# A planned kernel for an FFT mixer with a gated feed-forward: whole accumulator banks as the unit of a wait, no pauses in the weight preparation, a later deadline, longer loads

## The chip, the core and the metric

The kernel runs on one core of a Trainium2 chip. The core has a matrix engine (TensorE, called PE; its weight loads are listed apart as PEld), a vector engine (DVE), an activation engine (ACT), a general engine (POOL) and a queue that issues transfers (SP). Each takes its own instructions in the order in which the program holds them and waits for the others by semaphores. Matrix products land in accumulator banks (PSUM, 512 f32 values per partition and bank, eight banks), from which DVE and ACT read. The metric is the device time of one execution in microseconds.

## The reference, cut to what matters

For x of 8192 tokens by 448 channels, all in f32:

```
xn = layernorm(x)
s  = irfft2(soft(mlp2(relu(mlp1(rfft2(xn))))))   # complex block MLP over the frequencies, 4 blocks of 112 channels, soft threshold 0.01
g  = silu((gelu(xn @ w_gate) * (xn @ w_up)) @ w_down)   # 448 -> 1792 -> 448
out = x + s * g
```

The transform runs along the 8192 tokens only (the other spatial axis has length 1). It is computed as two stages of 128 and 64 points. Precision close to f32 comes from splitting every operand into two f16 parts and making three products of them.

## The kernel before

**Two streams.** The feed-forward (ffn() and chunk()) is the main stream on PE. It takes the 8192 tokens in 16 chunks of 512, twice: pass p=0 with the first 8 of the 14 column blocks of w_gate and w_up, pass p=1 with the other 6. The first two chunks of p=0 are computed plainly; every later one uses seven products instead of eight for the 2x2 block product of x with the weights (unit(), product()), on tokens and weights whose sums were made beforehand. Each chunk ends with its down projection onto 448 columns. Its partial result goes to DRAM (prt) in p=0 and is taken up again in p=1 (pt).

**The down projection** comes in two forms. The plain one, down(), is for each of four token tiles a run of 8 blocks x 3 matmuls of 448 columns in p=0. The other, down2() with prod2(), makes seven products instead of eight, of 224 columns each; it needs extra sums of the activations (sums() in unit(), which keeps them in the tiles "left" and "right" and in h) and factors of w_down (factors2(), factors_in()). chunk() chooses this form as soon as state holds "left", which prep_mlp() puts there with its last lines. At the start of the first such chunk, factors_in(0) loads the factors of w_down over the plain weights. All of p=1 uses it.

**The other stream** runs beside it in three phases. Phase 1 normalises x, makes the first transform stage (chunk1(), stage1()) and the sums of x; phase 2 (phase2(), group()) makes the second stage, the block MLP (layer1()), the threshold and the first inverse stage, in 16 groups of frequencies times 4 channel blocks, 64 in all; phase 3 (phase3(), tiles3(), load3()) makes the last inverse stage, multiplies with the gate and adds x. When phase 3 begins, chunks of p=1 that are past have left their gate in DRAM (gsp) and phase 3 reads it back, two loads for each; chunks that follow (from state["direct"] on) multiply at once, in gate().

**The weights** are prepared beside phase 1 by weights(): scaled, split and summed, for p=0 at the start and from some 150 us later for p=1 (gu_block() with 1), then the factors of w_down for p=1 (down_weights(1)) and for p=0 (factors0()), then the block MLP's weights (prep_mlp()).

**The order is planned while the program is built.** Pace is a small event simulation: every task is a generator that yields a time, an event, or nothing (wait until the last issued operation is done). issue() estimates the start and end of each operation and appends it to its engine's program at that moment, so the estimated times set the order in which instructions stand in each queue. They set nothing on the chip, where the semaphores rule. Four parts matter here:

- region(), ready() and note() say which earlier operations one has to wait for in the planner's model: operations on the same tensor whose column ranges overlap, a read only for writes, a write for both.
- The branch for SP in issue() estimates when a transfer has landed: 2.2 us and its size at 240 GB/s, or the end of the queue's traffic, and 2.5 us more for loads after 100 us.
- END2 and END3 are due times: phase 2 spaces the 64 groups evenly between its begin and END2, phase 3 its tiles between its begin and END3.
- calm() holds a task of the preparation back until its engine is free.

Rings (Ring.get and put) hand out buffers; a task without one waits. In layer1() one bank (BF) holds two sums: p0 in columns 0 to w and p1 in columns 256 to 256 + w. ACT copies p0 to k (common()), PE makes p1 meanwhile, DVE adds p1 to k (other()), and 1 us after the copy PE adds the third product to p0.

In the profile all operations carry line 200, the one line through which issue() records them, so they are told apart by their tiles: bx, by, bd and bf are the banks; wt and dw the weights; xta and xtb the transposed x; h the activations; z, zs, wn, vt and u belong to phase 2.

Of the kernel before, what the change touches and what calls it, by code (L numbers as in the profile page):

```python
# [16 lines left out]
PSUM = bass.MemoryType.PSUM  # L17
# [4 lines left out]
NG = 16  # L22
# [27 lines left out]
class Pace:  # L50
# [37 lines left out]
    def run(self):  # L88
        while self.heap:
            t, _, task = heapq.heappop(self.heap)  # L90
            self.now = max(self.now, t)
            self.last = self.now
            try:
                y = next(task)
            except StopIteration:
                continue
            if isinstance(y, Event):
                if y.done:
                    self.push(task, self.now)
                else:  # L100
                    y.waiting.append(task)
            else:
                self.push(task, self.last if y is None else max(self.now, y))


    @staticmethod
    def region(ap):
        dims = list(ap.ap)
        lo = ap.offset % max(1, dims[0][0])
        return ap.tensor.name, lo, lo + sum((n - 1) * s for s, n in dims[1:]) + 1  # L110
# [22 lines left out]
    def issue(self, e, op, out, ins, run):  # L133
        outs, ins, start = self.start(e, out, ins)
        if e == "SP":
            size = (outs or ins)[0].nbytes()
            self.dma = max(self.dma, start) + size / 320e3
            if op == "dma_start_transpose":
                self.free[e] = start + 1.15 + size / 380e3
                end = max(self.free[e] + 2.6, self.dma + 1.5)  # L140
            else:
                self.free[e] = start + 0.5
                end = max(start + 2.2 + size / 240e3, self.dma + 1.5) + (2.5 if outs and start > 100.0 else 0.0)
        else:
            end = start + self.cost(e, op, start, out, ins)
            self.free[e] = end
            if self.shares(e, op, out, ins):
                self.port[e] = self.port[e][-11:] + [(start, end)]
        for i in ins:
            self.note(i, False, end, e)  # L150
        for o in outs:
            self.note(o, True, end, e)
        self.last = max(self.last, end)
        return run()
# [233 lines left out]
def afno_geglu_kernel(ctx, tc, x, gu, wd, mlp, b1, b2, c_m, c_mt, c_small, out):  # L388
    nc = tc.nc
    pace = Pace()  # L390
# [86 lines left out]
    def ev(*key):  # L477
        return EV.setdefault(key, Event())

    def done(*key):  # L480
        pace.set(ev(*key))
# [176 lines left out]
    T1, DT = 84.0, 38.0  # L658


    def gu_loads(fs, again):
        for f in fs:
            t = yield from WS.get()
            if f < 4 and not again:
                yield 2.5 + 2.5 * f

            n = (8 if f < PF[0][1] and not again else SL) * 128
            Q.dma_start(t[:, 0:n], gu[f][:, 0:n])
            EV["wst", f, again] = t.rearrange("p (s c) -> p s c", s=SL)
            pace.then(lambda f=f: done("wl", f, again))  # L670
# [15 lines left out]
    def gu_block(b, to):  # L686

        f0, n = BLK[b]
        for i in range(n):
            yield ev("wl", f0 + i, 0)  # L690
            t = EV["wst", f0 + i, 0]
            yield from calm("DVE")
            V.tensor_reduce(fm[:, i, :, b], t[:, 0:8].rearrange("p (i k) f -> p i (k f)", i=2),
                            axis=AXIS.X, op=ALU.max, apply_absolute_value=True)
            yield
        mx = fx[:, :, b]
        if n == 2:
            V.tensor_tensor(mx, fm[:, 0, :, b], fm[:, 1, :, b], op=ALU.max)
        else:
            V.tensor_copy(mx, fm[:, 0, :, b])  # L700
        yield
        yield from largest(fx[:, :, NBK + b], mx, 2.0 ** -30)
        scales(b)
        yield
        scales_of_products(b)
        done("scales", b)
        for i in range(n):
            f = f0 + i
            t = EV["wst", f, 0]
            if to == 0:  # L710
                d, k = wt[f], 0
            else:
                d, k = (yield from WO.get()), 2
            yield from gu_split(f, t, d, k)
            done("w", f)
            if to == 0:
                WS.put(t)
            if i == 0:
                scale_of_gate(b)
            if to == 1:  # L720
                yield from gu_comb(f, t, d[:, :, 8 - k:16 - k])
                Q.dma_start(wsp[f - PF[1][0]], d.rearrange("p s v c -> p (s v c)"))
                WO.put(d)

    def gu_combs(fs):

        yield ev("w", 5)
        pace.spawn(gu_loads(fs, 1))
        for f in fs:
            yield ev("wl", f, 1)  # L730
            yield from gu_comb(f, EV["wst", f, 1], wt[f][:, :, 8:16])
# [53 lines left out]
    def factors2(p, j, v):  # L785

        f = PF[p][0] + 2 * j
        if block(f) == block(f + 1):
            yield from calm("ACT")
            S.activation(v, v, AF.Copy, scale=fd[:, 2, block(f):block(f) + 1])  # L790
        else:
            for e in range(2):
                yield from calm("ACT")
                S.activation(v[:, e], v[:, e], AF.Copy, scale=fd[:, 2, block(f + e):block(f + e) + 1])
        yield
        cb = yield from CB.get()
        c = cb.rearrange("p k c -> p (k c)")[:, 0:4 * DH].rearrange("p (k c) -> p k c", k=4)
        do = yield from WO.get()
        dv = do.rearrange("p s v c -> p s (v c)")[:, :, 0:7 * DH]
        b11, b12, b21, b22 = (v[:, e, DH * c_:DH * c_ + DH] for e in range(2) for c_ in range(2))  # L800
        yield from B.calm("tensor_sub", c[:, 0], b12, b11)
        yield from B.calm("tensor_sub", c[:, 2], b22, b12)
        yield
        yield from B.calm("tensor_sub", c[:, 1], b22, c[:, 0])
        yield
        yield from B.calm("tensor_sub", c[:, 3], b21, c[:, 1])
        yield
        cf = c.rearrange("p k c -> p (k c)")
        for k0, k1, src in ((0, 1, b11), (1, 3, v[:, 1]), (3, 7, cf)):
            yield from calm("ACT")  # L810
            S.copy(dv[:, 0, DH * k0:DH * k1], src)
            yield
            yield from B.calm("tensor_sub", dv[:, 1, DH * k0:DH * k1], src, dv[:, 0, DH * k0:DH * k1])
            yield
        CB.put(cb)
        Q.dma_start(dsp[p][:, :, 7 * DH * j:7 * DH * (j + 1)], dv)
        WO.put(do)

    def factors0(gap):
        for j in range(PF[0][1] // 2):  # L820
            yield pace.now + gap
            t = yield from WS.get()
            v = t[:, 0:2 * D].rearrange("p (t d) -> p t d", t=2)
            Q.dma_start(v, wd[256 * j:256 * j + 256, :].rearrange("(t p) d -> p t d", p=128))
            yield
            yield from factors2(0, j, v)
            WS.put(t)
# [1081 lines left out]

            pace.spawn(store())  # L1910

    END1, END2, END3 = T1 + NG * DT + 12.0, 1410.0, 1765.0

    def phase2():
        yield ev("phase1")
# [265 lines left out]
    def weights():  # L2181

        near = range(PF[0][1])
        t = yield from WS.get()
        Q.dma_start(t[:, 0:8 * 128], gu[1][:, 0:8 * 128])
        EV["wst", 1, 0] = t.rearrange("p (s c) -> p s c", s=SL)
        pace.spawn(gu_loads(near[2:], 0))
        for b in range(1, PB[0][1]):
            pace.spawn(gu_block(b, 0))
            if b == 1:  # L2190
                yield ev("scales", 1)
        combs = pace.spawn(gu_combs(near))
        yield ev("w", 1)
        yield pace.spawn(down_weights(0))
        yield combs
        yield 150.0
        for b in range(*PB[1]):
            yield pace.now + 10.0
            pace.spawn(gu_loads(range(BLK[b][0], sum(BLK[b])), 0))
            yield pace.spawn(gu_block(b, 1))  # L2200
        yield pace.now + 10.0
        yield pace.spawn(down_weights(1))
        yield pace.now + 10.0
        yield pace.spawn(factors0(10.0))
        yield pace.last + 5.0
        yield pace.spawn(prep_mlp())
        done("weights")
# [46 lines left out]
```

## Time and profile before

| | us |
|---|---|
| median of 3 runs | 1802.2 |
| lowest and highest | 1799.91, 1803.22 |
| the profiled execution | 1800.9 |
| its span in the trace | 1799.1 |

A line of instructions in order of time reads: start, duration, engine, line, operation, out<-in, shapes, count of merged instructions, and in brackets the idle time before it with what ended it. The duration of a merged line of matmuls runs to the modelled end of the last one, past the start of what follows, since matmuls overlap; the time that one takes of PE is read from the start of a run to the start of the next line. In a line of waits stand the engine and the tile, what it waited for, and then the total in us, the number of times and the longest. In a line of stages stand the stretch, its length, the busy time of each engine with its number of instructions, and then PE's granted clock as a share of full speed, the share of the 16 transfer engines that was busy, and GB/s.

### The profile page before, as it was taken

To read this page: it belongs to the slowest core of one execution; us is meant where nothing else is said; L and a number is where in the kernel's file an instruction comes from. 1 tells how busy PE (TensorE), PEld (TensorE's weight loads), DVE (VectorE), ACT (ScalarE), POOL (GpSimd) and SP (SyncE) were. 2 spreads that over 40 slices of the span, in tenths; PEclk is the share of its full clock that TensorE was granted. 3 is DMA by queue.
4 is the path that set the end of the run, shared out by engine and by line. 5 is a ranking of instruction groups with operands and counts; after the bars stand their busy time and mean duration, and the time that the engine had idled before them with its cause. 6 is when DMAs were issued, how large, how long until landed. Compare 5 with 4: busy or idle time off the path is not lost. (4 is left out here: it accounts for less than half of the span.)

```text
span 1799.1 us, 39944 instructions
## 1 busy us (share of the span) xinstructions
PE 1759.5 (98%) x16029; PEld 1457.2 (81%) x16029; DVE 1374.8 (76%) x2461; ACT 1012.0 (56%) x1977; POOL 521.5 (29%) x639
## 2 busy tenths in 40 slices
PE   7999999999999999999999999999999999999997
PEld 3446678776787777999999999899989998888887
DVE  7867778776776774777878787888788877888876
ACT  5745556555555544666767666676666653333333
POOL 3333344344433431122213133322223211221111
PEclk9999999999999999999999999999999999999999
DMA  6554775666656633523246555443344349989952
GB/s 219 160 152 126 201 213 158 197 212 185 192 157 202 198 108 107 143 63 73 52 104 197 156 119 120 108 100 95 98 120 117 77 117 305 290 244 287 295 175 63
DMA packets 353802, 283.51 MB, mean 158 GB/s; under 512 B 235120, under 2 KB 324464, under 8 KB 353616
## 3 DMA queue, kind: packets, MB, share of 16 engines
q1 hardware_dynamic: 353328, 280.41, 54.8%
q8 instruction: 125, 2.05, 0.5%
q14 instruction: 61, 0.50, 0.1%
q10 hardware_dynamic: 288, 0.56, 0.1%
HBM read 127.44 MB, written 104.32 MB: 129 GB/s over the span
## 5 line engine op out<-in xcount | busy, mean ns | idle before, releaser
L200 PEld LDWEIGHTS <-wt 128*128 128x128 f16 x9350 | 908.2, 98 | 173.3 <-issue 18.7
L200 PE MATMUL bx<-xta,wt 128*128 128x256 f16 (+1 forms) x3843 | 474.5, 275 | 2.0 <-ACT by L200 1.9
L200 PEld LDWEIGHTS <-h 128*128 128x128 f16 x2708 | 259.7, 98 | 98.4 <-issue 1.9
L200 PE MATMUL bd<-dw,h 128*128 128x448 f16 (+1 forms) x1704 | 283.5, 317 | 0.8 <-DVE pt L200 0.8
L200 PE MATMUL by<-xtb,wt 128*128 128x256 f16 x2080 | 250.9, 273 | 0.8 <-DVE by L200 0.8
L200 PE MATMUL by<-xta,wt 128*128 128x256 f16 (+1 forms) x1347 | 177.0, 281 | 5.3 <-DVE xta L200 3.1
L200 POOL TENSOR_TENSOR wt<-wt 128x256 f32<-128x256 f32 x84 | 67.0, 797 | 334.4 <-DVE wt L200 239.5
L200 PE MATMUL bx<-xtb,wt 128*128 128x256 f16 x1040 | 130.6, 273 | 2.7 <-DVE v L200 2.5
L200 DVE TENSOR_TENSOR by<-bx,u 128x512 f32<-128x512 f32 x104 | 72.4, 696 | 68.2 <-PE bx L200 59.0
L200 ACT COPY u<-by 128x512 f32<-128x512 f32 x104 | 60.8, 585 | 93.8 <-PE by L200 93.4
L200 PE MATMUL bd<-dw,wt 128*128 128x224 f16 (+1 forms) x816 | 99.5, 265 | 1.8 <-DVE pt L200 1.8
L200 ACT ACTIVATE u<-by,fc 128x512 f32<-128x512 f32 (+1 forms) x118 | 73.4, 634 | 49.2 <-PE by L200 48.9
L200 ACT CAST h<-wt 128x512 f16<-128x512 f32 (+1 forms) x128 | 68.4, 536 | 48.3 <-DVE wt L200 40.5
L200 DVE SCALAR_TENSOR_TENSOR pt<-bd,fb,pt 128x448 f32<-128x448 f32 (+1 forms) x97 | 64.8, 675 | 30.9 <-PE bd L200 30.1
L200 POOL TENSOR_TENSOR zs<-t,zs 112x256 f16<-112x256 f32 (+1 forms) x40 | 32.2, 804 | 187.1 <-ACT zs L200 160.7
L200 PE MATMUL bf<-w2t,wn 112*128 112x112 f16 x1512 | 84.8, 213 | 0.0
L200 DVE TENSOR_TENSOR v<-bx,u 128x512 f32<-128x512 f32 x104 | 71.2, 685 | 16.9 <-PE bx L200 16.2
L200 ACT COPY by<-bx 128x512 f32<-128x512 f32 x104 | 59.8, 575 | 40.9 <-PE bx L200 40.5
L200 PEld LDWEIGHTS <-wn 112*128 112x128 f16 x1512 | 80.3, 98 | 0.8
L200 ACT ACTIVATE th<-pt 128x448 f32<-128x448 f32 (+1 forms) x65 | 37.1, 570 | 76.8 <-DVE pt L200 65.9
L200 ACT ACTIVATE gl<-bx,fc 128x512 f32<-128x512 f32 (+1 forms) x70 | 40.5, 599 | 68.7 <-PE bx L200 59.2
L200 PEld LDWEIGHTS <-w1t 112*112 112x112 f16 x612 | 68.0, 130 | 9.8 <-DVE k L200 4.0
(240 smaller groups left out, 3159.4 us busy)
## 6 DMA issues: line engine op xcount, KB each, us to landing
xts<-sx SPq DMA_DIRECT2D x32, 480.0 KB, 3.3
x<-in_x SPq DMA_DIRECT2D x17, 896.0 KB, 6.3
t<-ysb SPq DMA_DIRECT2D x64, 224.0 KB, 2.9
prt<-th SPq DMA_DIRECT2D x64, 224.0 KB, 2.6
pt<-prt SPq DMA_DIRECT2D x64, 224.0 KB, 3.5
u<-t SPq DMA_DIRECT2D x32, 448.0 KB, 5.6
x<-in_x SPq DMA_DIRECT2D x32, 448.0 KB, 6.4
y<-t SPq DMA_DIRECT2D x30, 448.0 KB, 3.9
```

The source lines that it names most:

```text
L200: return self.pace.issue(self.name, kind, out, ins, lambda: fn(out, *args, **kw))
```

## The change

Four edits, all in what the planner is told; no operation's code is touched.

- region() gives every accumulator tensor the one range 0 to 1, so that any two accesses of a bank overlap.
- A load after 100 us is counted 3.0 us longer instead of 2.5.
- END2 is 1440 instead of 1410.
- In weights() the pauses of 10 us become 0: one before each of the three blocks of p=1, one before down_weights(1), one before factors0() and, through its argument, one before each of its four steps.

```diff
     @staticmethod
     def region(ap):
+        if ap.space == PSUM:
+            return ap.tensor.name, 0, 1
         dims = list(ap.ap)
...
-                end = max(start + 2.2 + size / 240e3, self.dma + 1.5) + (2.5 if outs and start > 100.0 else 0.0)
+                end = max(start + 2.2 + size / 240e3, self.dma + 1.5) + (3.0 if outs and start > 100.0 else 0.0)
...
-    END1, END2, END3 = T1 + NG * DT + 12.0, 1410.0, 1765.0
+    END1, END2, END3 = T1 + NG * DT + 12.0, 1440.0, 1765.0
...
         for b in range(*PB[1]):
-            yield pace.now + 10.0
+            yield pace.now + 0.0
             pace.spawn(gu_loads(range(BLK[b][0], sum(BLK[b])), 0))
             yield pace.spawn(gu_block(b, 1))
-        yield pace.now + 10.0
+        yield pace.now + 0.0
         yield pace.spawn(down_weights(1))
-        yield pace.now + 10.0
-        yield pace.spawn(factors0(10.0))
+        yield pace.now + 0.0
+        yield pace.spawn(factors0(0.0))
```

## The prediction

> **What bounds the kernel now.** I read the page's first part, then busy time by stage, then what TensorE (PE) waited for, then single stretches in order of time.
>
> ```profile
> span 1799.1 us, 39944 instructions
> PE 1759.5 (98%) x16029; PEld 1457.2 (81%) x16029; DVE 1374.8 (76%) x2461; ACT 1012.0 (56%) x1977; POOL 521.5 (29%) x639
> ```
>
> Stages, per line: PE, weight loads, DVE, ACT and POOL busy, PE's clock, DMA share, GB/s.
>
> ```profile
> 0.00:100.00 100.00, 83.58 (x421) 40.85 (x422) 81.73 (x185) 62.19 (x122) 34.61 (x47) 0.98 0.50 170
> 100.00:550.00 450.00, 447.42 (x3275) 319.42 (x3274) 327.49 (x569) 238.39 (x426) 184.91 (x254) 1.00 0.64 186
> 550.00:686.00 136.00, 136.00 (x1067) 104.57 (x1065) 98.45 (x175) 74.72 (x135) 50.28 (x68) 1.00 0.53 157
> 686.00:1475.00 789.00, 782.84 (x8411) 715.44 (x8410) 616.94 (x1126) 519.40 (x1090) 196.50 (x206) 1.00 0.42 107
> 1475.00:1740.00 265.00, 259.94 (x2396) 231.85 (x2394) 208.86 (x338) 95.92 (x169) 47.95 (x57) 1.00 0.91 275
> 1740.00:1800.00 60.00, 49.70 (x470) 45.06 (x467) 41.37 (x71) 21.38 (x38) 7.23 (x9) 0.94 0.22 62
> ```
>
> PE bounds it: 39.6 us idle in all, of which 16.4 lie in the start and 10.3 in the tail (0.9 of it past the span). Between them it idles 2.6 us (100 to 686), 6.2 (phase 2, to 1475) and 5.1 (phase 3, to 1740), with its clock at 1.00. So an edit can win by giving PE less work, or by taking part of these 13.9 us; everything on the other engines counts only through PE's waits. PE's waits in phase 2, and the largest two in phase 3 (total, times, longest):
>
> ```profile
> PE bf L200 <- DVE k L200: 5.7, 7, 1.4
> PE bx L200 <- DVE v L200: 0.5, 1, 0.5
> ...
> PE bx L200 <- ACT by L200: 1.9, 1, 1.9
> PE bd L200 <- DVE pt L200: 1.4, 6, 0.3
> ```
>
> **The pauses in weights().** Nine pauses of 10 us go (one before each of three blocks, one before down_weights, one before factors0 and four inside it), 90 us. The first p=0 chunk that finds the tile "left" made by prep_mlp uses seven products. Where the last of prep_mlp stands against chunk starts (a chunk starts with a bx matmul on xta behind a run of bd):
>
> ```profile
> 550.41 1.47 PE L200 MATMUL bx<-xta,wt 128*128 128x256 f16 x12
> ...
> 602.63 4.14 PE L200 MATMUL bd<-dw,h 128*128 128x448 f16 x21
> 606.61 1.47 PE L200 MATMUL bx<-xta,wt 128*128 128x256 f16 x12
> ...
> 659.56 1.28 DVE L200 SCALAR_TENSOR_TENSOR w2t<-raw,ms,w2t 112x448 f16<-112x448 f32 x2 [0.45 <-ACT w2t L200]
> 662.68 1.47 PE L200 MATMUL bx<-xta,wt 128*128 128x256 f16 x12
> ...
> L200 PEld LDWEIGHTS <-left x288: 95/98/101, 760.6 to 995.1; 128*128 128x128 f16 x144
> ```
>
> A seven-product chunk loads weights from "left" 72 times (products 3, 5 and 6, each 4 j x 2 halves x 3), so 288 is four chunks, 12 to 15. prep_mlp ends at 660.8 on the chip and chunk 11 starts at 662.7; the planner's own clock must have missed that start narrowly. With 90 us less it ends near 571: before chunk 10 (606.6), after chunk 9 (550.4). It takes 54 of the 90 us to reach chunk 10 and 110 to reach chunk 9, so exactly two more chunks, as the change says.
>
> What a chunk saves on PE: the run of 21 above goes from 602.63 to 606.61, 189.5 ns per 448-column matmul. The 224-column ones:
>
> ```profile
> 762.92 0.74 PE L200 MATMUL bd<-wt,h 128*128 128x224 f16 x6
> 763.50 0.74 PE L200 MATMUL by<-wt,h 128*128 128x224 f16 x6
> ```
>
> 0.58 / 6 = 96 ns. Eight products cost 4 token tiles x 8 blocks x 3 = 96 x 189.5 = 18.2 us; seven cost 7 x 4 x 2 x 3 = 168 x 96 = 16.1 us, and one 64-column matmul. 2.0 us per chunk, **-4.0 us** for two. Nothing on PE hides it: 550 to 686 is 136.00 of 136.00 busy.
>
> What could take it back: the extra sums and seven evictions in place of four on DVE, ACT and POOL. Their cover is DVE's slack, 27% in 550 to 686, where the weight work also leaves. A seven-product chunk beside phase 2 left PE no idle time:
>
> ```profile
> 716.00:784.00 68.00, 67.99 (x723) 62.79 (x722) 47.03 (x97) 41.06 (x90) 10.88 (x14) 1.00 0.44 117
> ```
>
> Squeezing the weight steps into 400 to 570 also raises DVE's 73% there, but each such operation is issued only when its engine is free, so an eviction waits at most for one of them. factors_in moves too: its 26 loads stand in SP's queue in chunk 10, with x loads and stores of phase 1 behind them, none needed by PE for a chunk or more. For all this I take 0; bounds -2.6 (all idle of 100 to 686 gone) and +2.6 (as much again).
>
> **Banks as the unit.** layer1 puts two sums in one bank: p0 in columns 0 to w, p1 from 256. One case in order of time:
>
> ```profile
> 1072.62 0.49 PE L200 MATMUL bf<-zs,w1t 112*112 112x256 f16 x3
> 1072.95 0.49 PE L200 MATMUL bf<-z,w1t 112*112 112x256 f16 x3
> 1073.28 0.49 PE L200 MATMUL bf<-zs,w1t 112*112 112x256 f16 x3
> 1073.48 0.37 ACT L200 COPY k<-bf 112x256 f32<-112x256 f32 x1
> ...
> 1076.20 0.41 DVE L200 TENSOR_TENSOR k<-bf,k 112x256 f32<-112x256 f32 x1
> 1076.67 0.49 PE L200 MATMUL bf<-z,w1t 112*112 112x256 f16 x3 [0.28 <-DVE k L200]
> ```
>
> The copy reads p0, complete before 1073.28, and starts behind p1's end (1073.44). The last product writes p0 and waits for DVE's read of p1. So on the chip a wait is already by bank; the old planner's region() let all three overlap. The edit adds and removes no instruction here: the planner now starts its copy one product (0.33 us, 1072.62 to 1072.95) later, and so places the last product later among PE's other work. Seven waits made the 5.7 us, 0.8 us each. Shortening each by 0.33 us gives 2.3; where DVE itself is late (here it came 2.4 us behind the copy) the new plan sees more of it. I take **-3.0 us**; bounds -6.2 (all of phase 2's idle) and +3 (as much again, since every order behind changes). What is queued behind the waiting product on PE is feed-forward work, which is what moves ahead of it. The other banks (halves of bx and by, two token halves of bd) are read whole already, so nothing there.
>
> A second kind of wait on a bank is in the trace, between two readers:
>
> ```profile
> 1058.19 0.57 ACT L200 ACTIVATE z<-bf 112x512 f16<-112x512 f32 x1
> 1058.66 0.37 ACT L200 ACTIVATE t<-bf 112x256 f32<-112x256 f32 x1
> 1059.06 0.69 DVE L200 SCALAR_TENSOR_TENSOR z<-bf,z 112x512 f16<-112x512 f32 x1
> ```
>
> DVE's z needs ACT's z (ends 1058.76), not t, yet it starts at 1059.06, right behind t's end (1059.03). The planner after the change still lets two readers of a bank overlap, since ready() makes a read wait for writes alone. If these uncounted waits are what makes DVE late, the 5.7 us stay: the second rival. The Trainium skill has this as a rule that speaks against the full gain (PSUM — Partial Sum Buffer, section "PSUM bank collisions raise a hardware error"): any two engines on one bank and quadrant have to be kept apart, reads against reads included. The trace agrees, with 0.03 us behind t against 0.30 behind z; by the rule alone the sum would be -4.0, by the seven waits shortened it is -7.0.
>
> **Deadline 1440 for 1410.** First and last group of phase 2:
>
> ```profile
> 746.13 0.83 PE L200 MATMUL bf<-sm,y 128*112 128x128 f16 x12
> ...
> 1439.65 0.67 PE L200 MATMUL bf<-sm,y 128*112 128x128 f16 x9
> ```
>
> 64 groups: 693.5 / 63 = 11.0 us each. The planner asks for about (1410 - 746) / 64 = 10.4, and will ask for 10.8. The pace kept is already slower than both, so its rings and engines set it, and I expect phase 3 to begin some 4 us later (bounds 0 and 30). It begins now at the very end of chunk 8 (SP):
>
> ```profile
> 1477.30 0.38 SPq L200 DMA_DIRECT2D u<-t  x1
> ...
> 1481.48 10.10 SPq L200 DMA_TRANSPOSE xta<-xts  x1
> ...
> gsp<-th SPq DMA_DIRECT2D x36, 224.0 KB, 2.6
> g<-gsp SPq DMA_DIRECT2D x18, 448.0 KB, 5.7
> ```
>
> Chunk 9 issues that transpose. 36 stores are four for each of nine chunks. PE reaches chunk 9 earlier and phase 3 comes later, so ten chunks go through gsp and five are gated at once: 0.9 MB more read in phase 3, 3 us of DMA time at 275 / 0.91 = 302 GB/s. PE, DVE and ACT do the same work per token either way. I take 0; bounds -1 and +20 (third rival).
>
> **Loads counted 0.5 us longer.** No wait of PE behind 100 us is for a DMA, so there is nothing to win; consumers are planned at most 0.5 us later and other work fills in. 0, bounds ±0.5.
>
> **Sum.** -4.0 - 3.0 = -7.0 on the profiled execution's 1800.9 (its span 1799.1 and 1.8 around it): 1793.9. The median shown, 1802.2, is 1.3 above that execution, so 1795.2 on its footing; I say 1795.
>
> **Rivals.**
> 1. The forecast, 1795 (own range 1791 to 1798.5): chance 0.50.
> 2. Only the shorter product count shows. For it: the uncounted readers; DVE, not the matmul order, was late at 1076. Against it: four of the seven waits would have to outlast a 0.33 us shift. 1802.2 - 4.0 = 1798: 0.20.
> 3. Slower: phase 3 becomes bound by transfers. It moves 0.91 x 265 = 241 us of full DMA now, 244 with the tenth chunk, and its end is held by END3. Once it begins later than 1740 - 244 = 1496, loads of u, mt and g land late, and the bf matmuls that read them stand in PE's in-order queue with the feed-forward behind them. A deadline that acts in full (1477 + 30 - 4 = 1503) is 7 us late at full use and 20 at 0.95; halfway 13, so 1802.2 - 7 + 13 = 1808. Against it: 11.0 us is the pace already. 0.12. By the Trainium skill (DMA: Bandwidth & Descriptors, section "Specifications") a core's HBM limit is some 358 GB/s, by which this stage's bytes (275 x 265 = 73 MB) take 204 us and this rival falls; the trace shows 302 at full share, which I go by.
> 4. More is won: phase 2's idle goes whole and half of the rest (2.6 + 5.1): -4.0 - 6.2 - 3.9 = 1788. 0.10.
> 5. The change doesn't do what it says: under 54 us of the 90 arrive (busy engines stretch the steps), one chunk or none changes: 1797 to 1799. 0.04.
> 6. The reordering makes as many new waits as PE gains: 1802. 0.04.
>
> **How the numbers follow.** About 0.2% (3.6 us) is what a measurement here tells from no change: faster is under 1798.6, slower over 1805.8. Faster: 0.95 of the first, 0.55 of the second, all of the fourth, half of the fifth: 0.475 + 0.11 + 0.10 + 0.02 = 0.70. Slower: the third and a little of the sixth, 0.13. Same: 0.17. The range takes the fourth at its edge and, upward, the sixth: 1788 to 1804.
>
> **What would show it.** Weight loads from "left" 288 to 432 (six chunks), 448-column bd matmuls 192 fewer, and the start of chunk 12 some 4 us earlier: first term. "PE bf <- DVE k" under 3 us: second. gsp stores 40, phase 3 within 10 us of 1477 less what was won, and its PE idle near 5 us: third. It is wrong if the left count stays, if phase 2's PE idle stays at 6 us, or if phase 3's grows past 10.

## The result and the profile after

The changed kernel takes 1789.1 us (median of 6 runs, 1787.3 to 1790.4) against 1801.5 for the kernel before (6 runs): a ratio of 0.9929, 95% interval 0.9916 to 0.9942. The profiled execution has a span of 1786.9 us, 12.2 less than before. In one of the runs below (readers) the profiled execution was granted a TensorE clock of 0.589 and is not read; the comparisons leave it out.

The first part of the page of the changed kernel, and its stages:

```profile
span 1786.9 us, 40239 instructions
PE 1754.2 (98%) x16175; PEld 1470.8 (82%) x16175; DVE 1398.0 (78%) x2492; ACT 1024.8 (57%) x2001; POOL 555.9 (31%) x670
```

```profile
0.00:100.00 100.00, 83.50 (x421) 40.88 (x422) 81.61 (x185) 62.21 (x122) 34.55 (x47) 0.98 0.49 170
100.00:550.00 450.00, 447.55 (x3275) 319.59 (x3274) 334.10 (x573) 245.43 (x437) 202.06 (x267) 1.00 0.67 194
550.00:686.00 136.00, 134.30 (x1136) 111.09 (x1136) 101.78 (x183) 72.58 (x140) 68.02 (x83) 1.00 0.54 155
686.00:1475.00 789.00, 788.25 (x8566) 730.07 (x8565) 634.41 (x1150) 530.20 (x1103) 202.81 (x216) 1.00 0.43 109
1475.00:1740.00 265.00, 261.50 (x2418) 233.96 (x2417) 210.94 (x344) 96.87 (x170) 41.99 (x51) 1.00 0.86 261
1740.00:1800.00 60.00, 39.14 (x368) 35.23 (x365) 35.14 (x61) 17.50 (x31) 6.49 (x8) 0.95 0.18 55
```

PE's idle time falls from 6.2 to 0.75 us in phase 2 (789 less the busy time) and from 5.1 to 3.5 in phase 3. Between 550 and 686, where it was nil, it is now 1.7. What PE waited for in phase 2 of the changed kernel is a single line; no wait for DVE's k is left:

```profile
PE bd L202 <- ACT th L202: 0.5, 1, 0.5
```

The unit of layer1 that the prediction shows with its wait (the 34th of 68 in both kernels), in order of time, after:

```profile
1072.17 0.49 PE L202 MATMUL bf<-z,w1t 112*112 112x256 f16 x3
...
1072.70 0.37 ACT L202 COPY k<-bf 112x256 f32<-112x256 f32 x1
...
1074.67 0.41 DVE L202 TENSOR_TENSOR k<-bf,k 112x256 f32<-112x256 f32 x1
...
1075.69 0.49 PE L202 MATMUL bf<-z,w1t 112*112 112x256 f16 x3
```

The copy still starts behind the second product's end, and DVE still reads p1 before the third product. But the third product now stands 0.61 us behind DVE's end (1074.67 + 0.41 = 1075.08), where it stood 0.06 behind it before (1076.67 for 1076.61), and other matmuls fill the time ahead of it, so nothing waits. The weight loads from "left" (first and last start follow the three durations), the turn to phase 3 in SP's queue, and the stores and loads of gsp:

```profile
L202 PEld LDWEIGHTS <-left x432: 95/98/121, 650.0 to 993.9; 128*128 128x128 f16 x144
```

```profile
1457.34 0.38 SPq L202 DMA_DIRECT2D u<-t  x1
...
1470.05 6.65 SPq L202 DMA_TRANSPOSE xta<-xts  x1
```

```profile
L202 SPq DMA_DIRECT2D gsp<-th x36: 536/541/585, 1045.6 to 1484.5; - x36
L202 SPq DMA_DIRECT2D g<-gsp x18: 327/401/543, 1462.4 to 1695.4; - x18
```

432 is 72 for each of six chunks, so six use seven products, as forecast. Phase 3 begins 20 us earlier than before (1457.3 for 1477.3), not 4 later, and it is still nine chunks that go through gsp.

**The account.** Idle time hides short gaps: the trace lists a 256-column matmul with 273 ns, though the next one starts 109 ns after it. So I count each matmul at its start-to-start time where nothing waits (189.5, 109, 96 and 49 ns for 448, 256, 224 and 112 columns; columns / 2.4 + 2.6 ns fits nearly all of these f16 matmuls, not the few in f32 or with 65 columns, which take longer: 51 ns for 65). The sum of these times is the "work", and the rest of a stretch is its "gap". In us, from the profiled execution of each kernel; the last column is from 1740 to the end:

| kernel | span | work | gap 0-100 | 100-686 | 686-1440 | 1440-1740 | tail |
|---|---|---|---|---|---|---|---|
| before | 1799.1 | 1745.2 | 27.3 | 1.7 | 7.5 | 6.3 | 10.1 |
| after | 1786.9 | 1741.2 | 27.3 | 3.8 | 0.4 | 4.6 | 8.3 |

Work is 4.0 less. The gap falls by 7.1 in phase 2 (686-1440), 1.7 in phase 3 (1440-1740) and 1.8 in the tail, and grows by 2.1 in phase 1 (100-686).

The gap can also be put down to places: what a matmul starts late, counted from the start of the one before and that one's free time, is charged to the late one. Of phase 2's gap, 7.2 us then stand before layer1's products out of z (bf<-z,w1t) in the kernel before, more than the 5.7 of listed waits, and 0.1 in the changed kernel.

In phase 1 two listed waits of PE are new. They are for xs, the two f16 parts of the normalised x, which the first transform stage reads:

```profile
PE bf L202 <- ACT xs L202: 1.0, 1, 1.0
PE bf L202 <- DVE xs L202: 1.0, 1, 1.0
```

### The profile page after: what moved, and what is told of

Same layout as the page of the kernel before. It is cut to its first block, busy times and chain, and to the rows that moved or that the text cites. A ratio compares the mean times of both kernels' runs of the same rounds, so it can differ in the third digit from the quotient of the medians.

```text
span 1786.9 us, 40239 instructions
## 1 busy us (share of the span) xinstructions
PE 1754.2 (98%) x16175; PEld 1470.8 (82%) x16175; DVE 1398.0 (78%) x2492; ACT 1024.8 (57%) x2001; POOL 555.9 (31%) x670
## 4 chain that ended last, share of the span: by engine, by line
PE 92%; DVE 5%; ACT 1%; DMA 1%; issue 1%; SPq 0%; POOL 0%; DVEq 0%; ACTq 0%; POOLq 0%
PE bx L202 30%; PE by L202 23%; PE bd L202 22%; PE bf L202 17%; DVE wt L202 1%; SPq L202 0%; DVE st L202 0%; DVE pt L202 0%; DVE x L202 0%; DVE fm L202 0%; DVE u L202 0%; POOL st L202 0%; DVE v L202 0%; DMA x<-in_x 0%; DVE h L202 0%
## 5 line engine op out<-in xcount | busy, mean ns | idle before, releaser
L202 PE MATMUL bd<-dw,h 128*128 128x448 f16 (+1 forms) x1596 | 253.4, 310 | 2.1 <-ACT th L202 1.0
L202 DVE SCALAR_TENSOR_TENSOR u<-by,fc,u 128x512 f32<-128x512 f32 (+1 forms) x86 | 55.5, 659 | 24.5 <-ACT u L202 11.7
L202 POOL TENSOR_TENSOR o<-o,c 128x448 f32<-128x448 f32 (+1 forms) x30 | 36.1, 1204 | 115.5 <-DVE c L202 96.0
```

The costliest lines, as they stand in the source:

```text
L202: return self.pace.issue(self.name, kind, out, ins, lambda: fn(out, *args, **kw))
```

## The experiments

The theory: two parts carry the gain, the two chunks' work and the banks, and the other two edits carry nothing. Its rivals: all of it comes from one part; spreading the groups by the deadline does what I put down to the banks; or any edit reshuffles an order of 40,000 instructions, and what is measured is the luck of the order. Each edit alone was put into the kernel before (first four), each alone was taken out of the changed kernel (next four), and four more followed. The ratio is always to the kernel before.

| kernel | ratio, 95% interval | span | work | 0-100 | 100-686 | 686-1440 | 1440-1740 | tail |
|---|---|---|---|---|---|---|---|---|
| s_bank | 0.9954 (0.9941-0.9967) | 1791.3 | 1745.2 | 26.9 | 0.0 | 1.8 | 7.8 | 8.4 |
| s_pauses | 0.9949 (0.9935-0.9963) | 1789.9 | 1741.2 | 27.1 | 2.9 | 3.9 | 3.9 | 9.7 |
| s_deadline | 0.9994 (0.9985-1.0003) | 1798.7 | 1745.2 | 28.4 | 1.7 | 9.0 | 3.7 | 9.7 |
| s_loads | 0.9976 (0.9967-0.9986) | 1797.2 | 1745.2 | 28.8 | 3.3 | 5.7 | 2.9 | 10.0 |
| x_bank | 0.9948 (0.9936-0.9960) | 1791.4 | 1741.2 | 26.7 | 1.8 | 6.7 | 4.1 | 9.6 |
| x_pauses | 0.9936 (0.9924-0.9949) | 1789.2 | 1745.2 | 27.1 | 0.6 | 3.2 | 3.8 | 8.1 |
| x_deadline | 0.9935 (0.9922-0.9949) | 1792.8 | 1741.2 | 29.1 | 6.3 | 0.9 | 5.4 | 9.0 |
| x_loads | 0.9911 (0.9898-0.9925) | 1785.6 | 1741.2 | 27.1 | 3.9 | 0.4 | 3.7 | 8.3 |
| bf_only | 0.9969 (0.9957-0.9981) | 1794.2 | 1745.2 | 26.7 | 1.6 | 1.8 | 7.5 | 10.1 |
| squeeze | 0.9960 (0.9948-0.9973) | 1793.5 | 1745.2 | 27.1 | 3.9 | 4.2 | 3.7 | 8.1 |
| readers | 0.9963 (0.9950-0.9977) | | | | | | | |
| three2 | 0.9928 (0.9915-0.9940) | 1788.1 | 1739.2 | 29.7 | 5.0 | 0.4 | 4.7 | 8.3 |

### One edit alone

s_bank, banks:

```diff
     def region(ap):
+        if ap.space == PSUM:
+            return ap.tensor.name, 0, 1
```

> The kernel before with one edit: accumulator banks as the unit of a wait. Theory (parts add): the matmuls in bf no longer wait for DVE's k, PE's idle time between 686 and 1475 us falls from 6.2 to under 2, ratio 0.9970 (-4 to -6 us). Rival (the gain of the change is the pauses alone): within 0.2% of before, the k waits stay near 5.7 us. Rival (luck of the order): the k waits go, but as much idle time turns up elsewhere, ratio 0.999 to 1.001.

The k waits fall to one, and phase 2's gap to 1.8:

```profile
PE bf L202 <- DVE k L202: 1.1, 1, 1.1
PE bd L202 <- ACT th L202: 0.8, 1, 0.8
PE bd L202 <- DVE pt L202: 0.2, 1, 0.2
```

8 us are won (0.46%), more than expected. Of them 5.7 lie in phase 2, 1.7 in phase 1 and 1.7 in the tail, which no theory had; phase 3's gap grows by 1.5.

s_pauses:

```diff
-            yield pace.now + 10.0
+            yield pace.now + 0.0
...
-        yield pace.spawn(factors0(10.0))
+        yield pace.spawn(factors0(0.0))
```

> The kernel before with one edit: no pauses in the weight preparation. Theory: two more chunks with seven products, weight loads from left 432, PE's work 4.0 us less and its waits as before, ratio 0.9978 (-4 us); the k waits stay between 4 and 7 us. Rival (the denser preparation costs PE what it saves): ratio 0.999 to 1.001 with PE idle before 686 us up by 3 or more. Rival (the whole gain of the change comes from here): 0.993.

The work falls by exactly 4.0. The gap before 686 grows by 1.2. Yet 9 us are won, since the gaps of phases 2 and 3, which this edit doesn't aim at, are 3.6 and 2.4 smaller; the k waits are less than half of before:

```profile
PE bf L200 <- DVE k L200: 1.8, 4, 0.9
...
```

I put that part, 6 us, down to the order's luck. The next two runs move the gaps of the same phases by 1.5 to 3.4 us without such an aim, and x_bank below, which has this edit too, is back at 6.7 in phase 2. That the whole 6 us are luck is not shown.

s_deadline and s_loads:

```diff
-    END1, END2, END3 = T1 + NG * DT + 12.0, 1410.0, 1765.0
+    END1, END2, END3 = T1 + NG * DT + 12.0, 1440.0, 1765.0
```

```diff
-                end = max(start + 2.2 + size / 240e3, self.dma + 1.5) + (2.5 if outs and start > 100.0 else 0.0)
+                end = max(start + 2.2 + size / 240e3, self.dma + 1.5) + (3.0 if outs and start > 100.0 else 0.0)
```

> The kernel before with one edit: END2 1440. Theory: nothing of its own, ratio 0.999 to 1.001, k waits near 5.7 us. Rival (spreading the 64 groups is what removes phase 2's waits): PE idle between 686 and 1475 us under 3, ratio 0.997. Rival (a later deadline only costs): phase 3 begins later, its PE idle time grows, ratio 1.002.

> The kernel before with one edit: loads counted 3.0 us longer instead of 2.5. Theory: nothing of its own, since no wait of PE is for a transfer; ratio 0.999 to 1.001. Rival (luck of the order): this edit, which should do nothing, moves the time by more than 0.2% either way, and then a shift of that size in any of the other runs proves nothing either.

The deadline alone does nothing: phase 2 keeps its gap (9.0) and 3.9 us of k waits, so spreading the groups doesn't remove the waits. The loads alone gain 0.24%, clear of zero, though before the edit no listed wait of PE behind 100 us was for a transfer. Its gap falls by 1.8 in phase 2 and 3.4 in phase 3 and grows by 1.6 in phase 1. So the luck rival holds at this size: an edit without a wait to act on, which only reshuffles the order, moves the time by some 4 us. That loads planned later help PE by way of another engine is not excluded by this run; x_loads below speaks against it.

### One edit taken out

x_bank, x_pauses, x_deadline and x_loads are the changed kernel with the diff of s_bank, s_pauses, s_deadline or s_loads undone.

> The changed kernel without the edit of the banks (pauses, deadline and loads changed). Theory: the k waits come back (4 to 7 us of PE idle between 686 and 1475 us), ratio to before 0.9965, against 0.9929 for the whole change. Rival (spreading the groups removes the waits, not the banks): under 2 us of k waits, ratio 0.993.

> The changed kernel with the pauses of 10 us put back (banks, deadline and loads changed). The planner's own clock has prep_mlp ready at 693 and phase 3 beginning at 1508 with ten chunks through gsp. Theory: four chunks with seven products again, 4 us more, ratio 0.9955. Rival 3 of the prediction (a late phase 3 is bound by transfers): PE idle between phase 3's begin and 1740 over 10 us and the DMA share near 1.0, ratio 1.000 or more.

> The changed kernel with END2 back at 1410 (banks, pauses and loads changed). Theory: the deadline gives nothing, ratio 0.993. Rival (spreading the groups gives part): PE idle between 686 and 1475 us back to 3 or more, ratio 0.9945 to 0.9955.

> The changed kernel with loads counted 2.5 us longer again (banks, pauses and deadline changed). Theory: ratio 0.993, as the whole change. Rival (luck of the order): off by more than 0.2%.

Without the banks the waits are back, and so is a phase 2 gap of 6.7 (0.9948):

```profile
PE bf L200 <- DVE k L200: 3.6, 4, 1.4
```

That is the second confirmation that the banks do it. Phase 2's gap is 7.5, 3.9, 9.0, 5.7 and 6.7 in the five kernels without the edit (mean 6.6) and 0.4, 1.8, 3.2, 0.9 and 0.4 in the first five with it (mean 1.3): 5.2 us. Of the later kernels with it, bf_only and three2 have 1.8 and 0.4, but squeeze has 4.2, above the lowest without the edit; there phase 2 runs on some 50 us longer. The part of the gap that stands before bf<-z,w1t tells the sets apart in every kernel: 7.2, 2.7, 5.2, 4.1 and 4.7 in the five without the edit, 0.1 to 2.2 in the eight with it (2.2 in squeeze).

Without the pauses' edit the ratio is 0.9936, 0.1% off the whole change: 4.0 us more work, but 3.2 less gap in phase 1. The two intervals overlap.

So the theory's parts do not add. Alone the banks win 0.46% and the pauses 0.51%; together, with the other two edits, 0.71%. Where they meet is phase 1. With the pauses kept, its gap is 0.0 and 0.6 in the kernels with whole banks (s_bank, x_pauses) and 1.6 to 3.3 in those without, bf_only among them. With the pauses gone it is 2.9 and 1.8 without the banks (s_pauses, x_bank), but 3.8, 6.3 and 3.9 with them (the changed kernel, x_deadline, x_loads). PE's waits for xs stand in these three and in squeeze, and in no other kernel whose profile is compared. So in these kernels the dense preparation costs PE that wait only in the company of the banks; why is not shown.

The run without the pauses' edit also has the late phase 3 of the prediction's third rival (its first load of u stands at 1494.4), with ten chunks through gsp and more transfers per us:

```profile
1500.00:1740.00 240.00, 237.41 (x2172) 210.09 (x2170) 196.39 (x318) 87.30 (x155) 47.49 (x53) 1.00 0.96 295
```

Transfers are busy for 0.96 of the time, and PE idles 2.6 us of 240. The rival's limit was a begin later than 1496; squeeze below is past it.

Deadline and loads: without either, the ratio is within 0.2% of the whole change. Alone, the loads' edit came with a shorter time; here the kernel without it is the faster one (0.9911 for 0.9929), though these two intervals overlap. The 0.24% that the loads won alone does not come again, so I don't count it as theirs.

### Where the banks act

bf_only, the edit on one kind of bank:

```diff
     def region(ap):
+        if ap.space == PSUM and ap.tensor.name.startswith('bf'):
+            return ap.tensor.name, 0, 1
```

> The kernel before with whole banks as the unit for the banks bf alone; bx, by and bd stay by column range. Theory: the bank edit works at two places, layer1 in bf (phase 2) and the two halves of the last chunk's bd (the tail). Then PE's gap in phase 2 is near 2 us as with the edit on all banks (1.8, against 7.5 before), and the tail keeps its old length of 9.6 to 10.1 us of gap instead of 8.1 to 9.0; ratio 0.9962. Rival: the tail was a matter of bf or of luck, 8.4, and the ratio is that of the whole edit, 0.9954.

Phase 2 has the whole effect (1.8) and the tail none (10.1). So the gain has two places. Phase 2 is bf; the tail is the other banks. There it can be read in order of time: the last chunk's last product is made in two halves of one bd bank. Before:

```profile
1789.76 0.44 DVE L200 SCALAR_TENSOR_TENSOR pt<-bd,fb,pt 128x224 f32<-128x224 f32 x1
...
1790.26 0.73 PE L200 MATMUL bd<-dw,h 128*128 128x224 f16 x6 [0.81 <-DVE pt L200]
...
1790.83 0.45 PE L200 MATMUL bd<-wt,h 128*128 128x224 f16 x3
1791.32 0.45 DVE L200 SCALAR_TENSOR_TENSOR pt<-bd,fb,pt 128x224 f32<-128x224 f32 x1 [1.11 <-PE bd L200]
1791.68 0.62 DVE L200 TENSOR_TENSOR th<-th,x 128x448 f32<-128x448 f32 x1
...
1792.22 0.85 DVE L200 TENSOR_TENSOR s<-pt,s 128x224 f32<-128x224 f32 x1
1792.99 1.22 DVE L200 SCALAR_TENSOR_TENSOR th<-th,s 128x448 f32<-128x448 f32 x3
...
1794.14 1.37 DVE L200 TENSOR_TENSOR th<-th,x 128x448 f32<-128x448 f32 x2
```

After:

```profile
1779.00 0.45 DVE L202 SCALAR_TENSOR_TENSOR pt<-bd,fb,pt 128x224 f32<-128x224 f32 x1
1779.36 1.19 DVE L202 TENSOR_TENSOR th<-th,x 128x448 f32<-128x448 f32 x1
...
1779.50 0.73 PE L202 MATMUL bd<-dw,h 128*128 128x224 f16 x6 [0.81 <-DVE pt L202]
...
1780.07 0.45 PE L202 MATMUL bd<-wt,h 128*128 128x224 f16 x3
1780.48 0.38 DVE L202 TENSOR_TENSOR s<-pt,s 128x224 f32<-128x224 f32 x1
1780.78 0.44 DVE L202 SCALAR_TENSOR_TENSOR pt<-bd,fb,pt 128x224 f32<-128x224 f32 x1
```

In both, PE's second half waits 0.81 us for DVE to read the first half of the bank. The old planner let them overlap, so it thought the second half early and queued DVE's read of it at once; DVE stood idle for 1.11 us with other operations behind it. The new one knows the wait and puts two of them ahead (th<-th,x and s<-pt,s). From the last run of matmuls to the span's end it is 8.3 us before (1790.83 to 1799.1) and 6.8 after (1780.07 to 1786.9). Every kernel with all banks has a tail of 8.1 to 9.0, every one without 9.6 to 10.1.

### The price of the dense preparation

squeeze, on x_loads:

```diff
-        if "left" in state and "seven" not in state:
+        if "left" in state and "seven" not in state and (p, i) >= (0, 12):
```

> Base: the changed kernel with loads counted 2.5 us longer (ratio 0.9911). One edit: seven products from chunk 12 on only, the pauses stay away, so the preparation is as dense but chunks 10 and 11 keep eight products. PE's work goes up by 4.0 us to 1745.2. Theory A (the denser preparation costs PE the 2 us more of gap before 686): the gap between 100 and 686 stays near 3.9. Theory B (the two chunks' extra sums cost it): the gap falls to 0 to 2. Either way the ratio is 0.992 to 0.994. The planner's clock now lets phase 3 begin at 1523 with ten chunks through gsp; rival 3 of the prediction (late phase 3 bound by transfers) would show as a gap of over 10 between 1440 and 1740.

The work goes back to 1745.2, and the gap between 100 and 686 stays at 3.9, as theory A had it. Between 550 and 686 PE is as idle as in the changed kernel, though DVE is less busy than in the changed kernel (101.78) or before (98.45):

```profile
550.00:686.00 136.00, 134.41 (x1048) 102.84 (x1047) 89.89 (x166) 67.14 (x122) 45.30 (x61) 1.00 0.48 139
```

So the extra sums of the two chunks cost PE nothing that shows. Taking the pauses out does, where the planner counts whole banks, by the density or by the order that comes with it, which this run doesn't tell apart. Phase 3 is late again: its first load of u stands at 1511.2, past the third rival's 1496 by 15 us. Its gap is 3.7, against 6.3 before, and its tail is as short as any (8.1). So that rival falls. The ratio, 0.9960, is outside what either theory expected (0.992 to 0.994); the span's surplus over x_loads, 7.9, is the 4.0 of work and 3.8 in phase 2's gap. Why phase 2 waits more there is not shown.

### Readers, and a third chunk

readers, on x_loads, lets the planner count one engine's read of a bank against another's:

```diff
         name, lo, hi = self.region(ap)
+        write = write or ap.space == PSUM
```

> Base: the changed kernel with loads counted 2.5 us longer (0.9911). One edit: the planner also lets a read of a bank wait for another engine's read of it. Theory (the uncounted readers are what keeps the rest of the gaps): PE's gap between 686 and 1740 falls from 4.1 to under 2, ratio 0.9895. Rival (after the change the readers no longer matter to PE): 0.990 to 0.992, gaps as they are. Rival (the planner grows too careful, its own end is 5 us later): ratio 0.993 or more.

0.9963: 0.5% slower than its base. The third outcome came; why is not shown. The rule of the Trainium skill that the prediction weighed (PSUM — Partial Sum Buffer, section "PSUM bank collisions raise a hardware error") asks that two engines' reads of one bank and quadrant be kept apart. The trace before agrees, with DVE's read 0.03 us behind the end of ACT's, but telling this planner of such waits doesn't help.

three2, on x_loads, issues the preparation's loads ahead instead of one step at a time:

```diff
-            pace.spawn(gu_loads(range(BLK[b][0], sum(BLK[b])), 0))
+            if b == PB[1][0]:
+                pace.spawn(gu_loads(range(PF[1][0], NF), 0))
...
-            if p == 1:
-                yield e
         yield e
...
-        for j in range(PF[0][1] // 2):
-            yield pace.now + gap
+        def one(j):
...
+        for e in [pace.spawn(one(j)) for j in range(PF[0][1] // 2)]:
+            yield e
```

> Base: the changed kernel with loads counted 2.5 us longer (0.9911). Edit: the loads of the weight preparation are issued ahead instead of one step at a time, so that prep_mlp ends before chunk 9 and three chunks, not two, get seven products more than before: weight loads from left 504, PE's work 1739.2. Theory (each chunk is worth 2.0 us of work less some 1.1 of new gap): ratio 0.9906. Rival (the preparation in 350 to 550 is now so dense that the gap before 686 grows by more than 2): 0.9915 or more.

The work falls by the 2.0 us of a seventh chunk, and the gap before 686 grows by 1.1, both as the theory has it. The ratio, 0.9928, is no better than x_loads' 0.9911 (the intervals overlap). Of the 2.5 us between the two spans, the first 100 us make up 2.6, where the clock differed (below), and phase 3 another 1.0; so whether a seventh chunk pays stays open. The fastest kernel of all is x_loads, 1787.4 us; it isn't told apart from the changed kernel's 1789.1.

## Why the prediction was right, and where not

1795 was forecast, 1789.1 measured: within the range of 1788 to 1804, but outside the forecast's own 1791 to 1798.5, on the side of more gain. The two parts it named carry most of the gain; how much each gives was in part missed, and in part balanced by luck.

- **The pauses, two more chunks, -4.0.** Exact: 432 loads, 1745.2 to 1741.2 of work.
- **The dense preparation, taken as 0** within ±2.6. It cost 2.1 in the pair. In the kernels with pauses the gap of phase 1 is 0.0 to 3.3 (mean 1.5 of six), without them 1.8 to 6.3 (mean 3.8 of six, three2 aside), and squeeze shows that it isn't the sums. The step argued about evictions alone ("an eviction waits at most for one of them"). The new listed waits, 2.0 us in the changed kernel, are no evictions but PE's for xs, the input of the first transform stage, and they come with the banks and the missing pauses together.
- **Banks in phase 2, -3.0.** That planning by banks takes the waits away held; the term was too small: -7.1 in the pair, -5.2 on average. I shortened each of seven waits by the 0.33 us of one product. In the unit shown, the third product stands no later behind the copy than before (2.99 us from start to start for 3.19), but DVE's add comes earlier (1.97 us behind the copy's start for 2.72). So moving the third product is not all that the edit does; how the rest comes about is not shown. And beside the listed waits stood gaps that no line listed: 7.2 us before bf<-z,w1t against 5.7 listed.
- **"The other banks ... are read whole already, so nothing there."** This step failed. The two halves of the last bd bank are not, and gave 1.5 us.
- **The deadline.** The step "I expect phase 3 to begin some 4 us later", with ten chunks through gsp, failed: 20 us earlier, nine chunks. It was read off the groups' pace, and I took that pace as fixed. The last matmul of bf<-sm,y, with which the last group starts, stands at 1440.1 before, 1421.9 in s_bank, 1427.1 in s_pauses and 1427.4 in the changed kernel, with the old deadline (x_deadline) at 1425.2: there the reordering sped the groups up, and the deadline hardly counted. Not everywhere: with the new deadline it stands at 1460.8 in x_pauses and at 1470.2 in squeeze, later than before, and why is not shown. The time was little touched by where phase 3 begins: its gap is 3.7 and 3.8 in squeeze and x_pauses, the two latest.
- **Loads, 0.** It holds in company (0.9911 without the edit, 0.9929 with it); the 0.24% that it moved alone I put down to the order.
- **Rivals.** The second (the waits stay, 1798) fell with the k waits. The third (phase 3 bound by transfers) fell in squeeze, where phase 3 begins 15 us past its limit; x_pauses, 2 us before the limit, agrees. The fourth, 1788, all of phase 2's idle and half of the rest, was nearest in the number. Half of it came: phase 2's idle went but for 0.75 us, while the rest did not shrink (100 to 686 rose from 2.6 to 4.2, phase 3 fell from 5.1 to 3.5). What made up for part of it is the tail, which that rival left out, so its nearness is luck in part.

Terms from the pair: -4.0 work, +2.1 phase 1, -7.1 phase 2, -1.7 phase 3, -1.8 tail: -12.5, against -12.2 in the span (matmuls across the bounds of a stretch make the difference). What the runs show to belong to the edits, by the means above, is -4.0 of work, +2.3 of phase 1, -5.2 of phase 2 and -1.5 of the tail, -8.4. The remaining 4 us are put down to the order's luck, whose size s_loads shows; no run isolates them, and their cause stays open.

## What to carry to other kernels

Where a planner sets the order, first compare the unit of its model's waits with the trace: an instruction that starts behind a matmul it doesn't need shows the real unit. Then look at every place where two parts of one bank are in flight; here two of them gained, one in the tail. Check edits in pairs: two that each win alone can meet in a third place and lose there. Price an edit of a planner by stage and by work, not by the whole time: here an edit without a wait to act on moved 0.24%. Idle time of 98% busy PE understates what can be won; count the matmuls at their free rate.

## What the runs showed of the hardware that was not expected

- With the same matmuls in the first 100 us, PE's gap there is 26.7 to 27.3 us in nine profiled executions and 28.4 to 29.7 in four. In just these four (s_deadline, s_loads, x_deadline, three2) the clock granted between 50 and 60 us was 0.83 to 0.88, in the nine 1.00. (Between 20 and 30 it was below 1 in all, 0.83, or 0.66 and 0.67 in three of the four.) It is the third number from the end in these rows of x_loads and three2:

```profile
50.00:60.00 10.00, 9.42 (x61) 4.78 (x60) 8.86 (x21) 8.64 (x21) 6.59 (x5) 1.00 0.70 216
```

```profile
50.00:60.00 10.00, 9.47 (x46) 4.13 (x47) 8.10 (x20) 8.18 (x20) 6.28 (x6) 0.83 0.62 177
```

  Executions of one kernel differ in this too: three of x_loads with a mean clock of 0.998 took 1786.6 to 1787.4 us, the one with 0.996 took 1789.3. All five of three2 had 0.996 or 0.997.

- Transfers can be busy for nearly all of a stage without PE waiting for them. The row of squeeze from 1520 on has a share of 0.98 at 304 GB/s, and PE is idle for 2.9 of 220 us:

```profile
1520.00:1740.00 220.00, 217.07 (x1980) 191.78 (x1979) 178.20 (x288) 80.11 (x141) 51.81 (x54) 1.00 0.98 304
```
